# Two halves of a filter unit multiplied at once, and transposes of 16 frequencies instead of 8

## The chip, the cores and the metric

The kernel runs on one core of a Trainium2 chip. A core has five engines that work side by side, each with its own queue of instructions carried out in order: TensorE (PE in the profile; its weight loads are listed apart as PEld), VectorE (DVE), ScalarE (ACT), GpSimd (POOL) and SyncE (SP), from whose queue most transfers between HBM and the on-chip memory SBUF are issued. [...] The metric is the time of one execution on the device in microseconds (us). Lower is better.

## The reference

Four layers act on x, 2048 rows (positions) by 512 channels, in float32. Each adds to x a function of the layer norm of x.

```python
x = x + _A_ref(_layernorm(x), A_w_r, A_w_i)
x = x + _B_ref(_layernorm(x), B_log_A_real, B_A_imag, B_C_real, B_C_imag, B_log_dt, B_D_skip)
x = x + _A_ref(_layernorm(x), A_w_r, A_w_i)
x = x + _B_ref(_layernorm(x), B_log_A_real, ...)

def _A_ref(x, w_r, w_i):                      # a filter in two-dimensional frequency space
    X = jnp.fft.rfft2(x, axes=(-2, -1)) * (w_r + 1j * w_i)
    return jnp.fft.irfft2(X, s=(S, D), axes=(-2, -1))

def _B_ref(u, log_A_real, A_imag, C_real, C_imag, log_dt, D_skip):
    dt = jnp.exp(log_dt)
    A = -jnp.exp(log_A_real) + 1j * A_imag
    C = (C_real + 1j * C_imag) * dt[:, None]
    P = jnp.exp((A * dt[:, None])[:, :, None] * pos)      # channel x mode x position
    K = 2.0 * jnp.einsum("dn,dnl->dl", C, P).real         # the filter from 128 modes
    ...                                                   # causal convolution of u with K by FFT
    return y + u * D_skip
```

The filter K of layer B is the same in both B layers. It has 2048 positions for each of 512 channels, and each value is a sum over 128 modes of a magnitude (a real exponential) times a cosine.

## The kernel before

All Fourier transforms are matrix products on TensorE, split into stages with small factors. The program computes the first A layer, then the first B layer in four blocks of 128 channels, then the second A layer and the second B layer. The filter K is made once, beside the first A layer and the first B layer, and its spectrum is kept for the second.

**The filter.** `kernel_time` goes through 32 units of 16 channels each; the 128 modes lie on the partitions. A position is written as a sum of a coarse and a fine part with 32 values each, so that a unit needs only factors of 16 channels x 32 values, and TensorE multiplies them out. A unit is worked in two halves of 8 channels. Its steps:

- `grow` (line 804), once a unit: three rows of magnitudes, `mag` with 3 x 512 elements, by exponentials on ScalarE and one product on GpSimd.
- `bend` (829), for each half: TensorE puts the phases into a PSUM bank (`pk`, two banks), VectorE rounds them (line 838), TensorE subtracts the whole turns (line 839).
- `sine` (842) and `cosine` (849), for each half: ScalarE takes the absolute value into `kf`, then a sine of the phase and a sine of the absolute value into a tile `qp` of 2 x 3 x 256 elements. All ScalarE work of these steps is recorded with one line, 800, that of the helper `ordered`, which also keeps their order.
- `terms` (853), for each half: VectorE makes two products of 256 elements (line 857, one reads its sine backwards) and one in place of 1024 elements (line 859) with the magnitudes.
- `total` (861), for each half: 16 small matmuls into the one PSUM bank `pv` (line 870), and a copy by ScalarE into `stage` (line 878). Full stages go to HBM.

The units are taken in groups of four (`GROUP`). Within a group the halves follow each other; `terms` lags `sine` by one half (`LAGT`), `total` by four (`LAGV`). After each group come the exponentials of the next, which need another table on ScalarE. `QP = 5` is the number of `qp` buffers, `MAG = 4` that of the magnitudes.

**The transposes.** `forward_b` (line 625) is the forward transform of a block of 128 channels, used for the filter itself (`kernel_freq`) and for the input of each B layer. `rows` makes 64 frequencies for all positions and ScalarE copies them out (line 648); `turn` (line 651) transposes eight of the 64 frequencies with one VectorE instruction of 512 elements (line 654); `pair` (line 659) runs the next matmuls of the helper `side_by_side` (line 316), each pair from 32 frequencies. `weigh` multiplies with the kept spectrum (line 962 from PSUM, line 974 sums of two SBUF tiles on VectorE or GpSimd), `back` transforms back.

**The order.** The lists of steps are dealt into each other by `interleave`, by fractions of each list: filter steps between steps of the layers. `layer_b` holds the transposes of the next block back in two halves of four, so that the first half stands at the end of one block and the second at the start of the next. On top of this written order a scheduler decides, when the program is built, in which order each engine's queue gets its instructions. Tiles come from pools with a fixed number of buffers; who takes a buffer waits for the last reader of its former content.

Of the kernel before, what the change touches and what calls it, by code (L numbers as in the profile page):

```python
# [11 lines left out]
ACT = mybir.ActivationFunctionType  # L12
ALU = mybir.AluOpType
# [36 lines left out]
WE2 = 'g'  # L50
MAG = 4
TH = 2
QP = 5
KF = 1
PM = '2,3,0'
WB = 7
# [190 lines left out]
class Net:  # L247
# [377 lines left out]
    def forward_b(self, src, T, tag="z", extra=None):  # L625


        nc = self.nc
        tiles = {}

        def rows(n0):


            if n0 == 0:
                tiles["z"] = self.sb("z", [64, 2, 2, 8, 2])
            xs = [src(n0 + i) for i in range(4)]
            ps = [self.ps("p1", [64, 2, 2, 2]) for b in range(2)]
            products = [(ps[b][64 * c:64 * c + 64, :, j, m], xs[2 * m + c][64 * b:64 * b + 64, 64 * j:64 * j + 64],
                         T[64 * b:64 * b + 64, n0 + 2 * m + c].rearrange("p (u r) -> p u r", r=2))
                        for m in range(2) for j in range(2) for c in range(2) for b in range(2)]  # L640
            if extra and n0 == 0:
                e = extra()
                for j in (1, 0):
                    products.insert(4 * j + 1, (ps[0][0:64, :, j, 0], e[:, 64 * j:64 * j + 64], products[0][2], True))
            self.side_by_side(products)
            m = n0 // 2
            for b in range(2):
                nc.scalar.copy(tiles["z"][:, :, :, b, m:m + 2].rearrange("p u j m r -> p (u j) (m r)"),  # L648
                               ps[b].rearrange("p u j m r -> p (u j) (m r)"))

        def turn(u):
            if u == 0:
                tiles["zt"] = self.sb(tag, [64, 2, 32])
            nc.vector.transpose(tiles["zt"][:, u:u + 8].rearrange("p u j d -> p (u j d)"),  # L654
                                tiles["z"][:, u:u + 8].rearrange("p u j b m r -> p (u j b m r)"))

        MB = split(self.small[:, 0:256], "slm", [2, 2, 64])

        def pair(i, use):
            last = None  # L660
            for pl in range(2):
                p = self.ps("p2", [512])
                products = []
                for h in (1, 0):
                    o = p[64 * h:64 * h + 64].rearrange("p (u d) -> p u d", d=32)
                    u = 32 * (i % 2) + 16 * h
                    c = 1 if u == 0 else 0
                    z = tiles["zt"][:, :, i // 2]
                    products += [(o[:, 0], MB[:, 0, pl], z[:, 0])] * c + [(o[:, c:], MB[:, 1, pl], z[:, u + c:u + 16])]
                last = self.side_by_side(products, last)  # L670
                use(pl, p)
            self.paired = last

        return ([partial(rows, n0) for n0 in range(0, 16, 4)], [partial(turn, u) for u in range(0, 64, 8)],
                [partial(pair, i) for i in range(4)])

    def exp(self, x, tmp):
# [99 lines left out]
    def kernel_time(self, parts, kt, units, group):  # L777

        nc = self.nc
        BF = mybir.dt.bfloat16  # L780
        TAU = 6.283185
        half = self.half
# [3 lines left out]
        live = {}  # L786
# [9 lines left out]
        def ordered(*a, **k):  # L796
            with ExitStack() as stack:
                if "x" in last:
                    stack.enter_context(self.tc.issue_after(last["x"]))
                last["x"] = nc.scalar.activation(*a, **k).ins  # L800

        last = {}
# [38 lines left out]

        def sine(i, j):
            p, mag = live[i, j]
            QP, f = self.sb("qp", [2, 3, 8, 32]), self.sb("kf", [512])
            ordered(f, p, ACT.Abs)
            ordered(QP[:, 1, 1:3].rearrange("p k d b -> p (k d b)"), p, ACT.Sin, scale=-TAU)
            live[i, j] = f, mag, QP

        def cosine(i, j):
            f, mag, QP = live[i, j]  # L850
            ordered(QP[:, 0, 1:3].rearrange("p k d b -> p (k d b)"), f, ACT.Sin, bias=half, scale=-TAU)

        def terms(i, j):
            f, mag, QP = live[i, j]
            m = mag[:, :, 256 * j:256 * j + 256].rearrange("p k (d b) -> p k d b", b=32)
            for c in (1, 0):
                nc.vector.scalar_tensor_tensor(QP[:, c, 0], QP[:, c, 1, :, ::-1], -1.0 if c else 1.0, m[:, 0], op0=ALU.mult, op1=ALU.mult)  # L857
            t = QP[:, :, 1:3].rearrange("p c k d b -> p c k (d b)")
            nc.vector.tensor_mul(t, t, mag[:, None, 1:3, 256 * j:256 * j + 256].to_broadcast([128, 2, 2, 256]))  # L859

        def total(i, j):

            h = i % 2
            QP = live.pop((i, j))[2]
            p = self.ps("pv", [2, 2, 64])
            for g in range(2):
                for c in range(2):
                    for t in range(2):
                        d = 4 * t + 2 * g
                        nc.tensor.matmul(p[64 * t:64 * t + 64, g], QP[:, c, 2, d:d + 2].rearrange("p s a -> p (s a)"),  # L870
                                         QP[:, c, 0:2, d:d + 2].rearrange("p k s b -> p s k b"),
                                         start=c == 0, stop=c == 1, tile_position=(0, 64 * t), skip_group_check=True)
            blk, ch = i // 8, i // 2 % 4
            if ch % 2 == 0 and h == 0 and j == 0:
                state["stage"] = self.sb("stage", [2, 64, 16])
            stage = state["stage"]
            k = 8 * (ch % 2) + 4 * h + 2 * j
            (nc.vector.tensor_copy if VC[(2 * i + j) % len(VC)] == "v" else nc.scalar.copy)(stage[:, :, :, k:k + 2], p.rearrange("p g s b -> p s b g"))  # L878
            if ch % 2 == 1 and h == 1 and j == 1:
                for t in range(4):  # L880
                    d = 128 * blk + 32 * t + 16 * (ch // 2)
                    self.dma("T")(kt.rearrange("(a b) d -> a b d", b=64)[:, :, d:d + 16],
                                      stage[32 * t:32 * t + 32, t % 2])
# [57 lines left out]
    def layer_b(self, kf, T, out, x=None, src=None, first=None, more=(), fill=(), switch=(), kept=None, fetch=None, after=None):  # L941
# [3 lines left out]
        nc = self.nc  # L945
# [68 lines left out]
            chain.insert(at, (None, *m))  # L1014
        if first is None:
            interleave(chain[0][1])
            interleave(chain[0][2][:4])
        turns = chain[0][2][4:] if first is None else []
        last = []
        fill = [*fill, *[[]] * len(chain)]  # L1020
        for i, (blk, _, _, pairs) in enumerate(chain):
# [9 lines left out]
            if tail:  # L1031
# [2 lines left out]


            steps = [[now[0], *turns, *last[:2]], [now[1], *last[2:4], *then[1][:1], *last[4:6]],
                     [now[2], *last[6:], *then[1][1:2], *units[:2]], [now[3], *units[2:4], *then[1][2:], *then[2][:4]]]
            turns, last = then[2][4:], [*units[4:], *rows]
            steps = sum(steps, [])
            half = len(steps) // 2  # L1040
            part = fill[i][:len(fill[i]) // 2], fill[i][len(fill[i]) // 2:]
# [2 lines left out]
            if tail:  # L1044
                keep = chain[-2][3]
                interleave(turns)
                interleave(chain[-2][1])
                interleave(last[:4])
                interleave(chain[-2][2][:4])
                fetch()  # L1050

                blk, _, _, pairs = chain[-1]
                now = [partial(weigh, blk, pairs, i, YC) for i in range(4)]
                interleave([keep[0], *chain[-2][2][4:], now[0], *last[4:6], keep[1], now[1], *last[6:], keep[2], now[2]])
# [42 lines left out]
def net_kernel(ctx, tc, x, w, ends, kin, log_dt, d_skip, out, **cst):  # L1097
# [15 lines left out]
    with ExitStack() as outer:  # L1113
        with ExitStack() as early:
            early.enter_context(net.phase("pk", P, pk=(2048, PK), pv=(2048, PV)))
            with net.phase("p", P, p1=(2048, 8 - PK - PV), p2="p1", p3="p1"), \
# [3 lines left out]
                with net.phase("m", side="right", raw=(8192, 1), val=(10240, 1), tmp=(14336, 1), hp=(5120, 2)):  # L1120
# [2 lines left out]
                    interleave(A[0][PC:], made)  # L1123
                net.end_weights(ends)
                early.enter_context(net.phase("k", side="right", kb=(5120, 1), ni=(256, 1), kw=(1024, 2), th=(1536, TH), mag=(6144, MAG),
                                              qp=(6144, QP), kf=(2048, KF), stage=(8192, 1)))
                K, marks = net.kernel_time(parts, kt, list(range(32)), GROUP)
                K = ahead(tc, K, KP)
                cuts = [round(f * len(K)) for f in FILL]
# [97 lines left out]
```

## Time and profile before

| | |
|---|---|
| runs, us | 785.32, 784.34, 794.32 |
| median, us | 785.32 |
| span of the profiled execution, us | 781.1 (its own time is given as this span only) |
| DVE busy | 649.3 us (83%) |
| PE busy, mean granted clock | 627.7 us (80%), 0.934 |
| ACT busy | 428.1 us (55%) |
| POOL busy | 404.9 us (52%) |

The profile is of one execution. Busy time is the time in which an engine had at least one instruction under way; for PE it includes waiting inside the matmul pipeline. A group of instructions is given with its line, engine, operation, written and read tiles, shapes and count, then busy time in us and the mean of one in ns, then the engine's idle time just before these instructions and who ended it. A row such as "A <- B: 6.9, 8, 1.9" in the list of waits reads: A waited for B 6.9 us in all, 8 times, at most 1.9 us at once. In the table of stretches each engine has its busy time in that stretch and, in brackets, how many instructions.

### The profile page before, as it was taken

How to read it: one execution, taken by the hardware profiler on the slowest of the kernel's cores; microseconds unless marked ns; L12 is line 12 of the kernel's file. 1: busy time of each engine (PE TensorE's matmuls, PEld its weight loads, DVE VectorE, ACT ScalarE, POOL GpSimd, SP SyncE). 2: the span in 40 equal slices, each digit the busy share in tenths (PEclk: the TensorE clock that was granted, in tenths of full speed). 3: DMA queues.
4: the chain of work that ended last, by engine and by line, in shares of the span. 5: the costliest groups of instructions: out<-in, count | busy, mean ns of one | idle time of the engine just before them, and what ended most of it. 6: DMA issues, size and time to landing. Idle time of an engine off the chain costs nothing. (4 is left out here: it accounts for less than half of the span.)

```text
span 781.1 us, 18929 instructions
## 1 busy us (share of the span) xinstructions
PE 627.7 (80%) x7248; PEld 443.5 (57%) x7248; DVE 649.3 (83%) x1301; ACT 428.1 (55%) x919; POOL 404.9 (52%) x596
## 2 busy tenths in 40 slices
PE   3447888897867977998889887874899896989986
PEld 2336666665534543656365656654777663566766
DVE  7998748979998999769996997878578696889992
ACT  3433778854748765887568834323756336242312
POOL 3675876764825245721657266281055572475760
PEclk9998899999979997999989999997999999799998
DMA  8300552344546503452325539422133114234513
GB/s 311 128 0 1 129 138 56 110 75 151 114 167 184 137 9 64 124 145 82 51 68 117 192 55 257 141 95 69 55 82 83 28 28 136 70 95 120 154 29 83
DMA packets 144923, 80.64 MB, mean 103 GB/s; under 512 B 78561, under 2 KB 124513, under 8 KB 143937
## 3 DMA queue, kind: packets, MB, share of 16 engines
q1 hardware_dynamic: 144576, 78.90, 36.2%
q8 instruction: 58, 0.95, 0.5%
q0 software_dynamic: 256, 0.52, 0.4%
q14 instruction: 33, 0.26, 0.1%
HBM read 54.89 MB, written 25.03 MB: 102 GB/s over the span
## 5 line engine op out<-in xcount | busy, mean ns | idle before, releaser
L974 POOL TENSOR_TENSOR u<-wb,wb 64x512 f32<-64x512 f32 x90 | 129.2, 1436 | 85.2 <-DVE wb L962 75.9
L316 PE MATMUL p<-z,mb 128*64 128x512 f32 (+2 forms) x480 | 102.0, 535 | 8.3 <-DVE wb L962 5.4
L870 PE MATMUL pv<-qp 128*64 128x128 f32 x1024 | 78.9, 295 | 11.4 <-DVE qp L859 6.9
L859 DVE TENSOR_TENSOR qp<-qp,mag 128x1024 f32<-128x1024 f32 x64 | 83.8, 1317 | 1.0
L962 DVE TENSOR_TENSOR wb<-p,kk 128x512 f32<-128x512 f32 x128 | 80.6, 674 | 4.7 <-PE p L316 4.6
L870 PEld LDWEIGHTS pv<-qp 128*64 128x64 f32 x1024 | 62.0, 147 | 38.8 <-ACT stage L878 10.2
L648 ACT COPY z<-p 128x512 f32<-128x512 f32 x96 | 51.4, 597 | 58.1 <-PE p L316 43.7
L316 PE MATMUL p<-mb,u 128*64 128x64 f32 x2048 | 72.9, 235 | 10.6 <-DVE u L974 4.5
L316 PEld LDWEIGHTS p<-mb,u 128*64 128x64 f32 x2048 | 70.7, 150 | 18.7 <-issue 11.3
L857 DVE SCALAR_TENSOR_TENSOR qp<-qp,mag 128x256 f32<-128x256 f32 x128 | 64.8, 523 | 13.6 <-ACT qp L800 13.3
L654 DVE STREAM_TRANSPOSE z<-z 128x512 f32<-128x512 f32 x96 | 58.5, 673 | 18.0 <-ACT z L648 18.0
L527 DVE TENSOR_TENSOR w<-wt,p 128x514 f32<-128x514 f32 x64 | 42.6, 686 | 33.3 <-PE p L316 18.6
L1086 POOL TENSOR_SCALAR w<-w,norms 128x128 f32<-128x128 f32 x64 | 40.5, 647 | 51.9 <-DMA w<-h 28.3
L532 POOL TENSOR_TENSOR w<-w,w 64x257 f32<-64x257 f32 x48 | 40.1, 835 | 50.3 <-DVE w L527 46.2
L456 PE MATMUL p<-w,w 128*128 128x128 f32 x128 | 32.0, 429 | 40.8 <-DVE w L449 30.8
L987 ACT COPY u<-p 128x512 f32<-128x512 f32 x64 | 37.6, 590 | 43.8 <-PE p L316 43.8
L316 PEld LDWEIGHTS p<-z,mb 128*64 128x64 f32 x480 | 34.2, 140 | 37.0 <-issue 20.2
L456 PEld LDWEIGHTS p<-w,w 128*128 128x128 f32 x128 | 27.8, 318 | 44.7 <-issue 24.8
L800 ACT ACTIVATE kf<-pk 128x512 f32<-128x512 f32 x64 | 38.9, 608 | 24.1 <-PE pk L839 23.6
L316 PE MATMUL p<-t,w 64*64 64x128 f32 x1024 | 43.3, 290 | 5.8 <-issue 2.6
L974 DVE TENSOR_TENSOR u<-wb,wb 64x512 f32<-64x512 f32 x38 | 46.9, 1234 | 0.5
L800 ACT ACTIVATE qp<-kf,half 128x512 f32<-128x512 f32 x64 | 47.2, 737 | 0.1
(200 smaller groups left out, 1495.3 us busy)
## 6 DMA issues: line engine op xcount, KB each, us to landing
wt<-in_w SPq DMA_DIRECT2D x32, 257.0 KB
kf<-kk SPq DMA_DIRECT2D x32, 256.0 KB
kk<-kf SPq DMA_DIRECT2D x32, 256.0 KB
u<-in_x SPq DMA_DIRECT2D x16, 256.0 KB
hr<-in_x SPq DMA_DIRECT2D x16, 256.0 KB
kt<-stage SPq DMA_DIRECT2D x32, 128.0 KB
h<-hr SPq DMA_DIRECT2D x16, 256.0 KB
w<-kt SPq DMA_DIRECT2D x32, 128.0 KB
```

The lines of the kernel that those rows point to most:

```text
L316: last = self.nc.tensor.matmul(out, weights, data, start=not more, stop=True, skip_group_check=True).ins
L456: nc.tensor.matmul(p[:, b], xf[:, b], t, start=True, stop=True)
L527: nc.vector.tensor_mul(m[pl], W, px[:, None, :].to_broadcast([128, 2, 257]))
L648: nc.scalar.copy(tiles["z"][:, :, :, b, m:m + 2].rearrange("p u j m r -> p (u j) (m r)"), ps[b].rearrange("p u j m r -> p (u j) (m r)"))
L654: nc.vector.transpose(tiles["zt"][:, u:u + 8].rearrange("p u j d -> p (u j d)"), tiles["z"][:, u:u + 8].rearrange("p u j b m r -> p (u j b ...
L800: last["x"] = nc.scalar.activation(*a, **k).ins
L857: nc.vector.scalar_tensor_tensor(QP[:, c, 0], QP[:, c, 1, :, ::-1], -1.0 if c else 1.0, m[:, 0], op0=ALU.mult, op1=ALU.mult)
L859: nc.vector.tensor_mul(t, t, mag[:, None, 1:3, 256 * j:256 * j + 256].to_broadcast([128, 2, 2, 256]))
L870: nc.tensor.matmul(p[64 * t:64 * t + 64, g], QP[:, c, 2, d:d + 2].rearrange("p s a -> p (s a)"), QP[:, c, 0:2, d:d + 2].rearrange("p k s b ...
L962: nc.vector.tensor_mul(split(m[c, pl], "du", [32, 16]), by_channel(p), split(k[c], "du", [32, 16]))
L974: self.added = e[0].tensor_sub(y[0:64], v[0, 0], v[1, 1]), e[1].tensor_add(y[64:128], v[0, 1], v[1, 0])
L1086: (self.nc.gpsimd if XNE[k] == "g" else self.nc.vector).tensor_scalar(t[:, k], t[:, k], scale, bias, op0=ALU.mult, op1=ALU.add)
```

## The change

Two edits. In the filter, both halves of a unit now share one `qp` tile of 2 x 3 x 512 elements. `sine` and `cosine` still run for each half and write their part of it; `terms` does nothing at the first half and at the second multiplies the whole unit: two products of 512 elements and one of 2048. `total` still runs for each half, on its part of the tile. There are three `qp` buffers of twice the size instead of five. In the transform, `turn` transposes 16 frequencies with one instruction of 1024 elements, and the lists of turns that the order deals out have half as many entries (two and two instead of four and four).

```diff
-QP = 5
+QP = 3
...
         def turn(u):
...
-            nc.vector.transpose(tiles["zt"][:, u:u + 8].rearrange("p u j d -> p (u j d)"),
-                                tiles["z"][:, u:u + 8].rearrange("p u j b m r -> p (u j b m r)"))
+            nc.vector.transpose(tiles["zt"][:, u:u + 16].rearrange("p u j d -> p (u j d)"),
+                                tiles["z"][:, u:u + 16].rearrange("p u j b m r -> p (u j b m r)"))
...
-[partial(turn, u) for u in range(0, 64, 8)]
+[partial(turn, u) for u in range(0, 64, 16)]
...
         def sine(i, j):
             p, mag = live[i, j]
-            QP, f = self.sb("qp", [2, 3, 8, 32]), self.sb("kf", [512])
+            if j == 0:
+                live[i, "qp"] = self.sb("qp", [2, 3, 512])
+            QP, f = live[i, "qp"], self.sb("kf", [512])
             ordered(f, p, ACT.Abs)
-            ordered(QP[:, 1, 1:3].rearrange("p k d b -> p (k d b)"), p, ACT.Sin, scale=-TAU)
+            ordered(QP[:, 1, 1:3, 256 * j:256 * j + 256], split(p, "kd", [2, 256]), ACT.Sin, scale=-TAU)
             live[i, j] = f, mag, QP

         def cosine(i, j):
             f, mag, QP = live[i, j]
-            ordered(QP[:, 0, 1:3].rearrange("p k d b -> p (k d b)"), f, ACT.Sin, bias=half, scale=-TAU)
+            ordered(QP[:, 0, 1:3, 256 * j:256 * j + 256], split(f, "kd", [2, 256]), ACT.Sin, bias=half, scale=-TAU)

         def terms(i, j):
+            if j == 0:
+                return
             f, mag, QP = live[i, j]
-            m = mag[:, :, 256 * j:256 * j + 256].rearrange("p k (d b) -> p k d b", b=32)
+            by_d = lambda t: t.rearrange("p (d b) -> p d b", b=32)
             for c in (1, 0):
-                nc.vector.scalar_tensor_tensor(QP[:, c, 0], QP[:, c, 1, :, ::-1], -1.0 if c else 1.0, m[:, 0], op0=ALU.mult, op1=ALU.mult)
-            t = QP[:, :, 1:3].rearrange("p c k d b -> p c k (d b)")
-            nc.vector.tensor_mul(t, t, mag[:, None, 1:3, 256 * j:256 * j + 256].to_broadcast([128, 2, 2, 256]))
+                nc.vector.scalar_tensor_tensor(by_d(QP[:, c, 0]), by_d(QP[:, c, 1])[:, :, ::-1], -1.0 if c else 1.0, by_d(mag[:, 0]),
+                                               op0=ALU.mult, op1=ALU.mult)
+            t = QP[:, :, 1:3]
+            nc.vector.tensor_mul(t, t, mag[:, None, 1:3].to_broadcast([128, 2, 2, 512]))

         def total(i, j):
-            QP = live.pop((i, j))[2]
+            QP = live.pop((i, j))[2].rearrange("p c k (d b) -> p c k d b", b=32)[:, :, :, 8 * j:8 * j + 8]
...
-            interleave(chain[0][2][:4])
-        turns = chain[0][2][4:] if first is None else []
+            interleave(chain[0][2][:2])
+        turns = chain[0][2][2:] if first is None else []
...
-                                              qp=(6144, QP), kf=(2048, KF), stage=(8192, 1)))
+                                              qp=(12288, QP), kf=(2048, KF), stage=(8192, 1)))
```

The other places where `layer_b` cuts a list of turns change in the same way, from 4 to 2.

More of the change, by code (lines that the diff above doesn't have):

```diff
@@ L672, in pair @@
             self.paired = last
-        return ([partial(rows, n0) for n0 in range(0, 16, 4)], [partial(turn, u) for u in range(0, 64, 8)],
+        return ([partial(rows, n0) for n0 in range(0, 16, 4)], [partial(turn, u) for u in range(0, 64, 16)],
                 [partial(pair, i) for i in range(4)])
@@ L1036, in layer_b @@
             steps = [[now[0], *turns, *last[:2]], [now[1], *last[2:4], *then[1][:1], *last[4:6]],
-                     [now[2], *last[6:], *then[1][1:2], *units[:2]], [now[3], *units[2:4], *then[1][2:], *then[2][:4]]]
-            turns, last = then[2][4:], [*units[4:], *rows]
+                     [now[2], *last[6:], *then[1][1:2], *units[:2]], [now[3], *units[2:4], *then[1][2:], *then[2][:2]]]
+            turns, last = then[2][2:], [*units[4:], *rows]
             steps = sum(steps, [])
@@ L1048, in layer_b @@
                 interleave(last[:4])
-                interleave(chain[-2][2][:4])
+                interleave(chain[-2][2][:2])
                 fetch()
@@ L1053, in layer_b @@
                 now = [partial(weigh, blk, pairs, i, YC) for i in range(4)]
-                interleave([keep[0], *chain[-2][2][4:], now[0], *last[4:6], keep[1], now[1], *last[6:], keep[2], now[2]])
+                interleave([keep[0], *chain[-2][2][2:], now[0], *last[4:6], keep[1], now[1], *last[6:], keep[2], now[2]])
                 units, rows = back(blk)
```

## The prediction

> **What bounds the kernel now.** I read the head of the page first, then a table of stretches, then the groups of VectorE (DVE) instructions, and last single stretches of the timeline. The chain that ended last came first only to be set aside: it covers the last 110 us, where the filter is long made.
>
> ```profile
> span 781.1 us, 18929 instructions
> PE 627.7 (80%) x7248; PEld 443.5 (57%) x7248; DVE 649.3 (83%) x1301; ACT 428.1 (55%) x919; POOL 404.9 (52%) x596
> ...
> PE 7%; DVE 5%; issue 2%; ACT 0%; DVEq 0%; ACTq 0%
> ```
>
> DVE is the busiest engine, TensorE (PE) stands right behind it. A mean over 781 us does not say which of them sets the pace where the change acts, so the next view cuts the part in which the filter is made (line 857's products run from 123.9 to 454.1 us, by a row quoted below) into stretches. The columns are the stretch, its length, and the busy time of each engine.
>
> ```profile
> core 0: us, PE busy (x) PEld busy (x) DVE busy (x) ACT busy (x) POOL busy (x), PEclk, DMA share, GB/s
> 116.00:160.00 44.00, 39.58 (x338) 29.26 (x338) 36.20 (x54) 37.75 (x87) 31.01 (x61) 0.96 0.25 76
> 160.00:240.00 80.00, 64.43 (x418) 40.38 (x418) 76.93 (x176) 46.37 (x90) 37.71 (x58) 0.89 0.47 128
> 240.00:280.00 40.00, 35.07 (x460) 20.70 (x459) 33.73 (x92) 32.58 (x64) 14.51 (x24) 0.96 0.56 149
> 280.00:320.00 40.00, 30.87 (x298) 17.69 (x298) 38.46 (x54) 22.04 (x41) 25.68 (x20) 0.83 0.25 48
> 320.00:360.00 40.00, 38.01 (x573) 25.95 (x572) 29.63 (x58) 33.24 (x65) 15.19 (x25) 1.00 0.52 138
> 360.00:400.00 40.00, 30.54 (x332) 16.83 (x331) 37.94 (x63) 26.39 (x49) 18.03 (x17) 0.94 0.27 56
> 400.00:440.00 40.00, 37.72 (x582) 26.20 (x583) 32.46 (x51) 32.14 (x63) 20.03 (x25) 0.93 0.49 131
> 440.00:480.00 40.00, 33.20 (x532) 23.45 (x531) 36.15 (x66) 17.18 (x35) 27.48 (x30) 0.91 0.54 129
> ```
>
> Two kinds of stretch alternate. In 160-240, 280-320, 360-400 and 440-480 (200 us together) DVE is busy 90 to 96% and PE about 80%: DVE sets the pace. In the other four (164 us) PE is busy 88 to 95%, ACT 80 to 86%, DVE 74 to 84%: there DVE work has cover, and a gain on DVE is worth nothing. Now the groups that the change touches (busy time, mean of one, idle time before them):
>
> ```profile
> L859 DVE TENSOR_TENSOR qp<-qp,mag 128x1024 f32<-128x1024 f32 x64 | 83.8, 1317 | 1.0
> L857 DVE SCALAR_TENSOR_TENSOR qp<-qp,mag 128x256 f32<-128x256 f32 x128 | 64.8, 523 | 13.6 <-ACT qp L800 13.3
> L654 DVE STREAM_TRANSPOSE z<-z 128x512 f32<-128x512 f32 x96 | 58.5, 673 | 18.0 <-ACT z L648 18.0
> ```
>
> They hold 207 of DVE's 649 us. The elements stay the same; what the change can save is what an instruction costs beside its elements.
>
> **The change part by part.** Removed: 64 of 128 short products (line 857), 32 of 64 long ones (line 859), 48 of 96 transposes (line 654): 144 instructions. Each survivor has twice the elements. What is one instruction worth? In a stretch without idle time the distance from start to start tells, not the duration, because neighbours overlap:
>
> ```profile
> 226.71 0.75 DVE L857 SCALAR_TENSOR_TENSOR qp<-qp,mag 128x256 f32<-128x256 f32 x2
> 227.38 0.68 DVE L339 BATCH_NORM_STATS2 bst<-hr 128x6 f32<-128x512 f32 x1
> ...
> 228.04 1.21 DVE L859 TENSOR_TENSOR qp<-qp,mag 128x1024 f32<-128x1024 f32 x1
> 229.18 0.67 DVE L601 TENSOR_TENSOR hr<-hr,p 128x512 f32<-128x512 f32 x1
> ...
> 331.32 4.86 DVE L654 STREAM_TRANSPOSE z<-z 128x512 f32<-128x512 f32 x8 [3.84 <-ACT z L648]
> ```
>
> Two short products take 227.38 - 226.71 = 0.67 us, 0.335 each; a long one 1.14. Then (1.14 - 0.335) / 768 elements = 1.048 ns an element, and 0.067 us is fixed. The transposes agree: 4.86 / 8 = 0.61 = 512 x 1.048 ns + 0.07. So the pure saving is 144 x 0.067 = 9.6 us of DVE time. The new pieces should take 0.60 us (short product, 512 elements), 2.21 (long, 2048) and 1.14 (transpose, 1024) from start to start.
>
> [...]
>
> Second, a wait. The view of one line gives shortest, median and longest duration in ns, and the first and last start:
>
> ```profile
> L857 DVE SCALAR_TENSOR_TENSOR qp<-qp,mag x128: 378/414/1495, 123.9 to 454.1; 128x256 f32<-128x256 f32 x128
> ...
> L859 DVE TENSOR_TENSOR qp<-qp,mag x64: 1185/1218/2301, 126.8 to 454.5; 128x1024 f32<-128x1024 f32 x64
> ```
>
> The means lie above the medians: 128 x (523 - 414) + 64 x (1317 - 1218) ns = 14.0 + 6.3 = 20.3 us are waits of single products. Where they arise:
>
> ```profile
> 295.20 4.32 POOL L974 TENSOR_TENSOR u<-wb,wb 64x512 f32<-64x512 f32 x3
> ...
> 297.17 1.22 DVE L857 SCALAR_TENSOR_TENSOR qp<-qp,mag 128x256 f32<-128x256 f32 x1 [1.51 <-ACT qp L800]
> 298.31 0.68 DVE L838 TENSOR_SCALAR kw<-pk 128x512 bf16<-128x512 f32 x1
> 298.92 0.89 DVE L857 SCALAR_TENSOR_TENSOR qp<-qp,mag 128x256 f32<-128x256 f32 x1
> 299.83 1.23 DVE L859 TENSOR_TENSOR qp<-qp,mag 128x1024 f32<-128x1024 f32 x1
> ```
>
> GpSimd (POOL) runs three sums of 1.44 us from 295.20 to 299.52. Each short product, which reads two SBUF tiles, ends about 0.3 us after one of those sums ends (298.08 and 299.52); the rounding of line 838, which reads PSUM, takes its usual 0.68. So a two-SBUF product waits out the GpSimd instruction under way. Half as many products meet half as many such waits if each product meets one by chance (10.1 us less), and no fewer if the GpSimd instructions are what is met (0 less). I take the first, since the waits fall on single products between other DVE work, and keep zero for the range.
>
> Of this, what lies in the DVE-paced stretches counts. Busy time there, of line 857, of line 859 and of the transposes:
>
> ```profile
> sum 200.00, DVE 37.31; mean DVE 9.33
> ...
> sum 200.00, DVE 43.46; mean DVE 10.87
> ...
> sum 200.00, DVE 12.06; mean DVE 3.02
> ```
>
> The shares are 37.31/64.8 = 0.58, 43.46/83.8 = 0.52, 12.06/58.5 = 0.21. Fixed part: (64 x 0.58 + 32 x 0.52 + 48 x 0.21) x 0.067 = 4.3 us. Waits: 7.0 x 0.58 + 3.2 x 0.52 = 5.7 us. Together -10.0 us. Behind the gain, PE at 80% comes next in those stretches, so 10 of 200 us fits under it.
>
> Third, what the merged form makes later. Products of a unit now begin only when the cosine of its second half is there, and one long product holds DVE 2.21 - 1.14 = 1.07 us longer at a time. Behind it on DVE's queue wait the roundings (line 838), for them PE's last phase matmul, for that ACT's next absolute value; and the sums on PE (line 870) wait for the product itself.
>
> ```profile
> ACT stage L878 <- PE pv L870: 33.9, 26, 4.8
> ...
> ACT kf L800 <- PE pk L839: 23.6, 21, 2.8
> ...
> PE pv L870 <- DVE qp L859: 6.9, 8, 1.9
> PE pk L839 <- DVE kw L838: 6.7, 7, 2.1
> ```
>
> In the built order a rounding stands directly behind a long product 13 times of 64 before and 10 times after. Bounds: nothing where other queued work fills the time; 10 x 1.07 = 10.7 us if each delay ends late. PE's waits on these two DVE results are rare now (15 in all, 0.9 us each), so I take a quarter, +2.7 us. The buffers cost nothing: three of two halves let ACT run as far ahead of PE's sums as five of one half (the sine of half n waited for the sums of half n-5; now the sine that opens unit i+3 waits for those of unit i, and its second half waits for nothing). ACT, PE, GpSimd and the DMA queues issue the same instructions as before, 921, 4010 and 601 on the first three; DMAs on SP change places by a few. At the four points where layer two's blocks begin, the built orders have emitted 32, 48, 64, 64 roundings before and 32, 49, 64, 64 after, so no work changes its stretch.
>
> Behind 480 us only transposes change. On the chain that ended last a block's transposes stand with two pieces or three (start, length):
>
> ```profile
> 667.32 1.20 DVE z L654 x2
> ```
>
> A block needs its second 16 frequencies first; four transposes of 0.60 are now two of 1.14, -0.13 us for each of four blocks: -0.5 us.
>
> Sum: -10.0 + 2.7 - 0.5 = -7.8 us. The profiled span becomes 773.3 us. The median of the runs, 785.3, lies 4.2 above the span; the profile gives no total for its own execution beside the span, and I keep that 4.2: 777.5, rounded to 777.
>
> **The rivals.** *Nothing gained* (780 to 788): GpSimd's instructions are met anyway, only 4.3 + 0.5 us come, and delays eat most: 785.3 - 4.8 + 2.7 = 783. For it: GpSimd is busy for 109 of the 200 DVE-paced us by the stretches. Against it: an undisturbed run of products has no such waits, and two of three instructions disappear from a half at once.
>
> *The whole saving comes through* (762 to 771): DVE sheds 9.6 + 10.1 = 19.7 us and all of it shortens the span, 785.3 - 19.7 = 766. For it: engines wait for each other in turns, and a DVE that is ahead may start PE earlier everywhere. Against it: 164 us with PE at 88 to 95%.
>
> *Slower: the unit waits for its second half* (788 to 810). The work is dealt in 8 groups of four units with a change of ACT's table between; each group's first sums now start one half later, and its last product ends 1.07 + 0.27 us later, while the next exponentials wait for the magnitude buffer that this product reads. A half lasts (454.1 - 123.9)/64 = 5.2 us. If that opening is uncovered in half of the groups, it costs 4 x 5.2 = 20.8 us, less the gains of 10.0 + 0.5 gives 785.3 + 10.3 = 796; in all eight, 816. It decides as soon as more than two groups are uncovered. For it: ACT already waits 33.9 us for sums. Against it: layer work is interleaved in every group.
>
> *GpSimd becomes late* (about 786 to 790): each of 32 long products can hold a GpSimd instruction 1.07 us longer. If eight such delays end PE's wait in the folding stage (160-240), 8.6 us eat the gain. [...] GpSimd's 48% idle time speaks against a loss.
>
> That the change does not do what it says can be left out: the built program has 64, 32 and 48 of the three instructions.
>
> **How the numbers follow.** Forecast (771 to 780): 0.45. Nothing gained, with GpSimd late: 0.25. Whole saving: 0.12. Slower by the second half: 0.18, two thirds of it above 801. A measurement of this kernel tells about 2% from no change: 769.6 and 801.0. Below: most of the third case, 0.10. Above: 0.12. Between: 0.78. The range leaves out the lower end of the third and the upper half of the fourth: 765 to 800.
>
> **What would show it.** Short products near 0.68 us and long ones near 2.28, undisturbed; their excess over this near 10 us in all; DVE busy time down 18 to 22 us; DVE-paced stretches shorter by some 5%, the others unchanged; and the time after 540 us within 1 us. Wrong it would be if PE's and ACT's waits for products and roundings rise by more than 10 us, or if the excess stays at 20 us.

## The result

The changed kernel is slower: 804.49 us median (801.35 to 809.31, 6 runs) against 786.73 us (779.09 to 794.32, 6 runs) for the kernel before; the ratio is 1.0274 [1.0228, 1.032]. The forecast was 777 us, its range 765 to 800.

First the head of the page of the changed kernel, with the span and the busy time of each engine:

```profile
span 804.7 us, 18753 instructions
PE 637.9 (79%) x7247; PEld 451.4 (56%) x7248; DVE 631.2 (78%) x1157; ACT 429.3 (53%) x919; POOL 417.2 (52%) x596
```

DVE does its work in 631.2 us instead of 649.3, with 144 instructions fewer, and yet the span of the profiled execution is 23.6 us longer (the medians lie 17.8 us apart). The groups of DVE instructions that the change touches, and the roundings behind them (busy time, mean of one in ns, idle time before them and who ended it):

```profile
L654 DVE STREAM_TRANSPOSE z<-z 128x1024 f32<-128x1024 f32 x48 | 55.6, 1212 | 26.9 <-ACT z L648 26.7
L864 DVE TENSOR_TENSOR qp<-qp,mag 128x2048 f32<-128x2048 f32 x32 | 74.1, 2316 | 0.8
L838 DVE TENSOR_SCALAR kw<-pk 128x512 bf16<-128x512 f32 x64 | 43.0, 680 | 29.2 <-PE pk L836 29.2
L861 DVE SCALAR_TENSOR_TENSOR qp<-qp,mag 128x512 f32<-128x512 f32 x64 | 51.0, 818 | 12.8 <-ACT qp L800 12.7
```

The view of one line, for the two products (shortest, median and longest duration in ns, first and last start):

```profile
L861 DVE SCALAR_TENSOR_TENSOR qp<-qp,mag x64: 649/685/1756, 130.1 to 469.2; 128x512 f32<-128x512 f32 x64
L864 DVE TENSOR_TENSOR qp<-qp,mag x32: 2267/2285/3025, 133.4 to 470.8; 128x2048 f32<-128x2048 f32 x32
```

The instructions are as short as forecast. Their waits for GpSimd come to 64 x (818 - 685) + 32 x (2316 - 2285) ns = 9.5 us, 20.3 before. So nothing went wrong with these instructions themselves; the time is lost elsewhere. The table of stretches of the changed kernel, at four places (the same columns as before):

```profile
160.00:240.00 80.00, 63.30 (x432) 42.72 (x431) 66.03 (x139) 45.07 (x89) 42.83 (x63) 0.93 0.44 113
280.00:320.00 40.00, 29.15 (x223) 15.38 (x223) 35.92 (x42) 21.70 (x39) 23.84 (x17) 0.74 0.20 35
320.00:360.00 40.00, 34.37 (x529) 23.44 (x523) 23.55 (x27) 29.88 (x59) 16.84 (x23) 0.91 0.47 124
400.00:440.00 40.00, 28.13 (x420) 19.68 (x421) 29.84 (x31) 25.12 (x49) 26.34 (x24) 0.87 0.33 82
```

In 160-240 DVE is busy 66.03 of 80 us, 76.93 before: room, but no earlier end. In 400-440 no engine is busy three quarters of the time, where PE had 37.72 of 40: engines wait for each other in turns. A fixed cut doesn't compare shifted kernels, so the next table cuts at line 962 (967 after), the products with the filter's spectrum, 16 to a block: at the end of the first, 17th, 33rd and 49th of them.

| part, us | before | after |
|---|---|---|
| until the first block's products | 285.2 | 284.8 |
| first block to second | 91.7 | 106.5 |
| second to third | 85.9 | 93.4 |
| third to fourth | 33.7 | 37.0 |
| from there to the end | 284.7 | 282.9 |

Units 0 to 15 and the folding of the filter lose nothing, the layers after the filter nothing; the blocks beside which units 16 to 31 are made lose 25.6 us. Each column is one execution, and differences of a few us mean nothing: E4 below, whose VectorE order is that of the kernel before, takes 4.6 us longer up to the first block. The list of waits of the changed kernel:

```profile
ACT stage L883 <- PE pv L875: 45.2, 31, 6.5
ACT kf L800 <- PE pk L839: 35.7, 25, 4.5
DVE kw L838 <- PE pk L836: 29.2, 13, 8.3
PE pk L839 <- DVE kw L838: 12.1, 9, 4.0
```

Against 33.9, 23.6, 1.6 and 6.7 before. All four have grown; which of them costs time, only experiments tell.

### The profile page after: what moved, and what is told of

The parts are those of the page before. It is cut to its first block, busy times and chain, and to the rows that moved or that the text cites. A ratio compares the mean times of both kernels' runs of the same rounds, so it can differ in the third digit from the quotient of the medians.

```text
span 804.7 us, 18753 instructions
## 1 busy us (share of the span) xinstructions
PE 637.9 (79%) x7247; PEld 451.4 (56%) x7248; DVE 631.2 (78%) x1157; ACT 429.3 (53%) x919; POOL 417.2 (52%) x596
## 5 line engine op out<-in xcount | busy, mean ns | idle before, releaser
L979 POOL TENSOR_TENSOR u<-wb,wb 64x512 f32<-64x512 f32 x90 | 135.9, 1510 | 113.5 <-DVE wb L967 105.6
L316 PE MATMUL p<-z,mb 128*64 128x512 f32 (+1 forms) x480 | 104.2, 542 | 6.6 <-DVE wb L967 3.3
L875 PEld LDWEIGHTS pv<-qp 128*64 128x64 f32 x1024 | 65.1, 153 | 33.6 <-issue 15.0
L654 DVE STREAM_TRANSPOSE z<-z 128x1024 f32<-128x1024 f32 x48 | 55.6, 1212 | 26.9 <-ACT z L648 26.7
L864 DVE TENSOR_TENSOR qp<-qp,mag 128x2048 f32<-128x2048 f32 x32 | 74.1, 2316 | 0.8
L532 POOL TENSOR_TENSOR w<-w,w 64x257 f32<-64x257 f32 x48 | 44.0, 916 | 51.8 <-DVE w L527 47.9
L1091 POOL TENSOR_SCALAR w<-w,norms 128x128 f32<-128x128 f32 x64 | 36.9, 589 | 56.6 <-DMA w<-h 48.8
L838 DVE TENSOR_SCALAR kw<-pk 128x512 bf16<-128x512 f32 x64 | 43.0, 680 | 29.2 <-PE pk L836 29.2
L861 DVE SCALAR_TENSOR_TENSOR qp<-qp,mag 128x512 f32<-128x512 f32 x64 | 51.0, 818 | 12.8 <-ACT qp L800 12.7
L800 ACT ACTIVATE kf<-pk 128x512 f32<-128x512 f32 x64 | 38.5, 602 | 36.7 <-PE pk L839 35.7
L316 PEld LDWEIGHTS p<-z,mb 128*64 128x64 f32 x480 | 35.0, 141 | 37.6 <-issue 20.2
L979 DVE TENSOR_TENSOR u<-wb,wb 64x512 f32<-64x512 f32 x38 | 50.3, 1323 | 0.7
```

Source lines behind the costliest of these rows:

```text
L316: last = self.nc.tensor.matmul(out, weights, data, start=not more, stop=True, skip_group_check=True).ins
L532: e[0].tensor_sub(Y[0:64, v], m[0][hs, 0], m[1][hs, 1])
L654: nc.vector.transpose(tiles["zt"][:, u:u + 16].rearrange("p u j d -> p (u j d)"), tiles["z"][:, u:u + 16].rearrange("p u j b m r -> p (u j ...
L838: nc.vector.tensor_scalar(whole, p, MAGIC, -MAGIC, op0=ALU.add, op1=ALU.add)
L861: nc.vector.scalar_tensor_tensor(by_d(QP[:, c, 0]), by_d(QP[:, c, 1])[:, :, ::-1], -1.0 if c else 1.0, by_d(mag[:, 0]), op0=ALU.mult, op1= ...
L864: nc.vector.tensor_mul(t, t, mag[:, None, 1:3].to_broadcast([128, 2, 2, 512]))
```

## The experiments

All ratios are to the kernel before, with 95% intervals; points are per cent of its time.

**One edit at a time.** E1 has the merged products with transposes of 8, E2 the transposes of 16 with products by halves.

```diff
 E1: QP = 3, sine, cosine, terms, total as changed;  turn(u): u:u + 8, as before
 E2: turn(u): u:u + 16, lists of turns cut at 2;     QP = 5, kernel_time as before
```

> The products for both halves at once, transposes of 8 frequencies as before. If the loss comes from the products (late start, long instruction or buffers): ratio to before 1.02 to 1.03, VectorE's wait for its rounding near 29 us. If it comes from the transposes: 1.00, wait near 2 us.

> Only the transposes of 16 frequencies; products and buffers as before. If the transposes do the harm: 1.02 or more. If the products do it: 0.995 to 1.00, with some 3 us of VectorE time saved, of which 0.5 to 1.5 us show behind 540 us.

E1 measured 1.011 [1.0071, 1.0149], E2 1.0025 [0.9991, 1.0058]. The products lose by themselves, though less than the 1.02 expected. The transposes alone can't be told from no change, but both together lose 1.4 points more than the sum.

**Late, or merged?** E4 keeps the shared tile of a unit, three buffers, and makes the products of each half at their old place. E3 also has products of the old size, but the first half's are issued behind the second half's.

```diff
 E4:
+        def terms(i, j):
+            half_terms(i, j)          # 2 products of 256, 1 of 1024, on half j of the tile
 E3:
+            if j == 0:
+                return
+            half_terms(i, 0, half_terms(i, 1))
```

> One tile for a unit, products of the old sizes (256 and 1024 elements), but those of the first half issued behind those of the second. Tells late start from long instruction. Late start (the first half's products wait for the second half's cosine): 1.02 to 1.035, a little worse than the merged products, since the 144 fewer instructions are not had. Long instruction (one product holds VectorE 2.2 us): 1.00 to 1.01.

> One tile for a unit and three buffers of it, products of the old sizes at their old places; VectorE's order is that of the kernel before. Buffers or the shared tile as the cause: 1.02. Late start or long instruction as the cause: 1.00.

E3 measured 1.0326 [1.0291, 1.036], E4 0.9984 [0.9938, 1.0031]. So three big buffers cost nothing, and a late start with 128 + 64 products and no merged instruction costs 3.4 points, about 27 us. From E3 to E1 the merging gives 2.1 points back, about 17 us. Not all of this need be the saving: E3's order also makes PE wait longer for the products, as its list of waits shows:

```profile
PE pv L886 <- DVE qp L869: 16.2, 14, 3.8
```

The same wait is 6.9 us before and 3.0 in E1.

**At the ends of a group?** Groups of four units with a change of ACT's table between (1283 ns for one load at line 800 of the kernel before, 16 in all) were the place that the prediction's slower rival named. E5 makes the first unit of each group by halves and merges the others, E6 does that with the last unit, E7 with both.

```diff
+            if i % group == 0:                  # E5;  E6: group - 1;  E7: in (0, group - 1)
+                return half_terms(i, j)
```

> Transposes of 8. The first unit of each group of four makes its products half by half as before; the other three units at once. If the harm lies in the opening of a group (no products to do before the second half's cosine): the 1.011 of the merged products falls to 1.000 or below. If it lies in the closing (the magnitudes and sums of the last unit come late): it stays near 1.011. If every unit pays alike: a quarter comes back, 1.008.

> Transposes of 8. Only the last unit of each group half by half, the other three at once. Closing: 1.000 or below. Opening: near 1.011. Every unit alike: 1.008.

> Transposes of 8. First and last unit of each group half by half, the two in the middle at once. Opening and closing together: 0.993 to 0.998, below the kernel before, since the middle units keep half of the saved instructions. Every unit alike: 1.005.

Measured: E5 1.0083 [1.0048, 1.0119], E6 1.0151 [1.0105, 1.0197], E7 1.0152 [1.0102, 1.0202]. The intervals of E5 and E6 both hold E1's 1.011, so neither end of a group can be told from nothing, and E7, which merges only two units of four, is no faster than E1: it missed both of the values expected. The loss doesn't come back with the openings and closings, and it isn't a sum over units.

**Which units?** E9 merges units 0 to 15 and leaves 16 to 31 by halves, E10 the other way round.

```diff
+            if i >= 16:                         # E9;  E10: i < 16
+                return half_terms(i, j)
```

> Transposes of 8. Units 0 to 15, whose products mostly lie beside the first A layer, at once; units 16 to 31, beside the blocks of the B layer, half by half. If merging pays where the filter has slack and costs only in the blocks, where each block waits for its filter: 0.993 to 0.999. If the cost is spread over all units: 1.005.

> The other way round: units 16 to 31 at once, units 0 to 15 half by half. Cost in the blocks only: 1.012 to 1.018, all of it between the first and the last spectrum product of the first B layer. Cost spread over all units: 1.005.

E9 measured 0.9972 [0.993, 1.0014], E10 1.0176 [1.0127, 1.0226]. The loss belongs to units 16 to 31, beside the blocks, as the table of parts said: in E10's profiled execution (794.76 us, below its median of 801.61) the three parts from the first block to the fourth take 12.8 us longer than before, the whole span 11.8. In E10 it can be watched. From the timeline of E10, VectorE (start, length, and in brackets the idle time before with its releaser):

```profile
315.43 1.26 DVE L990 TENSOR_TENSOR u<-wb,wb 64x512 f32<-64x512 f32 x1
316.62 3.41 DVE L872 SCALAR_TENSOR_TENSOR qp<-qp,mag 128x512 f32<-128x512 f32 x2
320.07 2.29 DVE L875 TENSOR_TENSOR qp<-qp,mag 128x2048 f32<-128x2048 f32 x1
322.28 1.28 DVE L838 TENSOR_SCALAR kw<-pk 128x512 bf16<-128x512 f32 x2
328.97 1.30 DVE L872 SCALAR_TENSOR_TENSOR qp<-qp,mag 128x512 f32<-128x512 f32 x2 [5.41 <-ACT qp L800]
```

And from E10's timelines of GpSimd, TensorE and ScalarE in the same window:

```profile
314.88 4.61 POOL L990 TENSOR_TENSOR u<-wb,wb 64x512 f32<-64x512 f32 x3 [4.14 <-DVE wb L978]
...
323.02 0.59 PE L839 MATMUL pk<-kw,ni 128*128 128x512 bf16 x1 [7.04 <-DVE kw L838]
...
323.70 0.60 ACT L800 ACTIVATE kf<-pk 128x512 f32<-128x512 f32 x1 [7.29 <-PE pk L839]
```

PE's phases (lines 835 and 836) had been issued by 314.1. The roundings that they wait for stand on DVE's queue behind three products: the two short ones take 3.41 us instead of 1.30, because they meet GpSimd's three sums, the long one 2.29. In that time PE's queue stands at line 839, and the matmuls of the back transform stand behind it, though they need no rounding and GpSimd's last sum for them was ready at 319.49. ACT has nothing to do until the phases come; then DVE, with its products done, waits 5.41 us for ACT's sines. One delay is paid by three engines in a row. At this place the kernel before has a single rounding between products, and on PE's queue the 64 matmuls of the back transform stand ahead of line 839; from the timelines of its VectorE and TensorE:

```profile
317.10 0.67 DVE L838 TENSOR_SCALAR kw<-pk 128x512 bf16<-128x512 f32 x1
...
318.79 1.50 DVE L857 SCALAR_TENSOR_TENSOR qp<-qp,mag 128x256 f32<-128x256 f32 x1
320.21 0.67 DVE L838 TENSOR_SCALAR kw<-pk 128x512 bf16<-128x512 f32 x1
...
316.64 3.46 PE L316 MATMUL p<-mb,u 128*64 128x64 f32 x64 [0.70 <-ACT u L983]
320.04 0.53 PE L839 MATMUL pk<-kw,ni 128*128 128x512 bf16 x1
```

So PE's order changed here too, and no run tests that by itself.

The changed kernel shows the same one block later, where the roundings stand behind the short products; the timeline of its VectorE:

```profile
416.44 3.42 DVE L861 SCALAR_TENSOR_TENSOR qp<-qp,mag 128x512 f32<-128x512 f32 x2
419.79 1.27 DVE L838 TENSOR_SCALAR kw<-pk 128x512 bf16<-128x512 f32 x2
...
436.97 1.29 DVE L838 TENSOR_SCALAR kw<-pk 128x512 bf16<-128x512 f32 x2 [8.29 <-PE pk L836]
438.18 4.61 DVE L654 STREAM_TRANSPOSE z<-z 128x1024 f32<-128x1024 f32 x4
```

and its TensorE:

```profile
420.51 1.19 PE L839 MATMUL pk<-kw,ni 128*128 128x512 bf16 x2 [3.96 <-DVE kw L838]
```

**Roundings first.** If the order on DVE's queue is the cause, merged products should cost nothing once the rounding stands ahead of them. E12 is E1 with each unit's short products issued only behind the newest rounding; E12A is the same on the changed kernel, with transposes of 16. E15 puts the same rule on the kernel before. The rule is two edits: `LAGT = 2` deals the products out one half later, and `issue_after` holds the short ones back. They were not tried apart.

```diff
-LAGT = 1
+LAGT = 2
...
-            nc.vector.tensor_scalar(whole, p, MAGIC, -MAGIC, op0=ALU.add, op1=ALU.add)
+            last["round"] = nc.vector.tensor_scalar(whole, p, MAGIC, -MAGIC, op0=ALU.add, op1=ALU.add).ins
...
+                with self.tc.issue_after(last["round"]):
                     nc.vector.scalar_tensor_tensor(...)
```

> Products at once, transposes of 8; each unit's products are issued on VectorE only behind the newest rounding, so that no rounding stands behind a late product. If the loss is the rounding behind the products (TensorE's queue stands, ScalarE has no phases): 0.995 to 1.003 in place of 1.011, VectorE's wait for products' sines grows instead. If it is the late start itself: 1.011 or more.

> The same on the changed kernel with its transposes of 16. Rounding behind products as the cause: 1.000 to 1.010 in place of 1.027. Late start: 1.025.

> The kernel before, whose products are also issued only behind the newest rounding. If putting roundings ahead is worth something by itself: 0.985 to 0.99, and the products at once with roundings ahead would still lose beside it. If it only mends what the late products do: 1.00 to 1.01, since here products that are ready are held back.

E12 measured 0.9986 [0.9952, 1.002], E12A 1.003 [0.9998, 1.0063], E15 1.0263 [1.022, 1.0305]. The loss is gone, in E12 from 1.011 and in E12A from 1.0274. One thing came out against the expectation: VectorE's wait for the products' sines, 9.5 us in E1 and 12.7 in the changed kernel, didn't grow in E12 but vanished. So the rule changes two things at once, what stands behind late products and VectorE's waiting in front of them, and E12 alone doesn't tell which of them counts; the kernel before has 13.3 us of the second and loses nothing. It isn't that this order is better for any kernel: on products by halves it costs 2.6 points, more than either value expected. Why it costs there wasn't tried; such a product waits for a rounding 64 times instead of 32, and ACT waits 44.9 us for PE's phases, longer than in the changed kernel. Under the same rule the merged form is 1.0263 / 0.9986, 2.8 points or 22 us, the shorter one. E12's list of waits:

```profile
ACT stage L884 <- PE pv L876: 53.1, 37, 6.5
DVE kw L838 <- PE pk L836: 23.9, 15, 4.0
ACT kf L800 <- PE pk L839: 20.2, 20, 4.2
...
PE pk L839 <- DVE kw L838: 5.6, 5, 1.9
```

The conspicuous new wait, DVE for PE's phases (29.2 us after, 1.6 before), stays at 23.9 in a kernel that loses nothing, and ACT's wait for the sums even grows: neither total follows the loss. The two that fall back are PE's for the rounding and ACT's for PE behind it (35.7 after, 23.6 before, 20.2 here). The latter in the list of waits of E4, which loses nothing either:

```profile
ACT kf L800 <- PE pk L839: 23.2, 25, 2.5
```

and in that of E1:

```profile
ACT kf L800 <- PE pk L839: 40.4, 26, 6.9
```

Totals over the whole run don't settle it: E2 loses nothing measurable with 30.5 us of this wait and 10.2 of PE's for the rounding, and E6 loses 1.5 points with 30.3 and 6.7. The list of PE's waits over the first two blocks alone separates better. The row of PE's wait for the rounding there, of the kernel before, the changed kernel and E10, in this order:

```profile
PE pk L839 <- DVE kw L838: 3.9, 4, 2.1
PE pk L839 <- DVE kw L838: 10.1, 6, 4.0
PE pk L839 <- DVE kw L838: 12.6, 6, 7.0
```

In the first two blocks of E12 it is 2.6 us and of E9 3.4, without a loss; of E1 6.9 and of E15 8.9, with one; only E2 has 6.2 without one. Directly this wait is 6 of the 25.6 us that the blocks lose. PE also waits longer there for ACT's sines to free a phase bank (4.8 us before, 9.5 after) and for transfers of the filter (1.5 and 6.4), and from the first block to the fourth it is busy 189.5 us instead of 178.0. That all of this follows from the roundings is argued, not shown.

The corresponding place of E12 in the timelines of its VectorE and TensorE:

```profile
323.84 1.27 DVE L838 TENSOR_SCALAR kw<-pk 128x512 bf16<-128x512 f32 x2
325.04 1.27 DVE L862 SCALAR_TENSOR_TENSOR qp<-qp,mag 128x512 f32<-128x512 f32 x2
326.34 3.25 DVE L865 TENSOR_TENSOR qp<-qp,mag 128x2048 f32<-128x2048 f32 x1
...
324.56 0.38 PE L839 MATMUL pk<-kw,ni 128*128 128x512 bf16 x1 [1.09 <-DVE kw L838]
```

The long product still takes 3.25 us, but PE waits 1.09 us and not 7.04.

**Another way out: a third phase bank.** If PE's phases were merely too few ahead, a third `pk` bank would help (one bank is taken from the other matmul results for it).

```diff
-PK = 2
+PK = 3
...
-PM = '2,3,0'
+PM = '2,2,0'
```

> The kernel before with three phase banks instead of two, and one bank less for each of two stages of the transforms. A base for the next run; 1.00 to 1.03 for the bank that the transforms lose.

> Products at once, transposes of 8, three phase banks. If the two banks tie rounding, sine and product into a ring that the late products stretch: at or below the run before, a loss of 0 instead of 1.1 per cent. If the banks play no part: 1.011 times the run before.

With three banks the kernel before measured 1.0133 [1.0092, 1.0175], E1's products 1.0295 [1.0251, 1.034]. The merged form still loses 1.0295 / 1.0133 = 1.016: the number of banks is not what the loss hangs on.

**What the transposes add.** E8 is the changed kernel with lists of turns of the old length, every second one empty.

```diff
         def turn(u):
+            if u % 16:
+                return
...
-[partial(turn, u) for u in range(0, 64, 16)]
+[partial(turn, u) for u in range(0, 64, 8)]
```

> Products at once and transposes of 16, as in the changed kernel, but the lists that the order deals out keep eight entries of transposes, every second one empty. If the transposes harm through the places that the shorter lists give to the filter's steps (roundings of the next group ahead of the transposes near 430 us): 1.010 to 1.015 in place of 1.027. If through their length: 1.027.

It measured 1.0225 [1.016, 1.0291], between E1 and the changed kernel, and its interval overlaps that of the latter: this settles nothing. In its trace the four transposes of that block stand ahead of the next roundings again (at 433.92, as in E1 at 433.28; after: 438.18). That with the roundings first both sizes of transposes are alike (E12, E12A) suggests that most of the 1.4 points hangs on the late products too.

**Versions that might beat both.** E11 is E9 with transposes of 16 in the second B layer alone, E16 is E12 with the same, and E17 is E12 with the rule on units 16 to 31 alone.

```diff
 E11, E16:
+    def forward_b(self, src, T, tag="z", extra=None, n=8):      # n=16 where layer two's input is transformed
 E17:
+                    if i >= 16:
+                        stack.enter_context(self.tc.issue_after(last["round"]))
```

> Units 0 to 15 at once as in the run before last, and transposes of 16 frequencies in the second B layer alone, where no filter is made. 1 to 1.5 us below that run: 0.991 to 0.998. If the longer transposes cost by themselves: above it.

> Products at once behind the newest rounding, transposes of 8 beside the filter and of 16 in the second B layer alone: 0.996 to 0.999, some 1 us below the same without the long transposes.

> Products merged, transposes of 8, and a unit's short products issued on VectorE only behind the newest rounding, but for units 16 to 31 alone, those beside the first B layer's blocks. Theory (the late products stand ahead of the rounding only there): units 0 to 15 keep what merging gives them in the built order, so at least as good as the same rule for all units: 0.994 to 0.999 of the kernel before. Rival (the rounding has to come first in the folding stage too): 1.000 to 1.006.

E11 measured 0.9998 [0.9964, 1.0032], E16 1.0032 [1.0002, 1.0062], E17 0.9962 [0.9924, 1.0] (medians of 785.27 us and, before, 785.53). Transposes of 16 gain nothing measurable even where no filter work is about; E11 and E16 both missed the gain of some 1 us. E17 is the best median beside E4's, and not told apart from the kernel before. DVE is busy 631.2 us in E12, 629.0 in E12A and 628.5 in E17, 18 to 21 us less than before, and no version is shorter for it. Whether some lateness that remains eats the saving, or DVE's time is worth nothing there, no run separates.

## Why the prediction was wrong

**What bounds the kernel: right as a reading, too strong as a rule.** The stretches where DVE is busy 90 to 96% were there. But before the first block DVE's busy time fell from 244.4 to 230.7 us, and that part is 284.8 us long instead of 285.2. The scheduler used the room for something else: before the first block PE did 448 of the filter's matmuls (line 870) instead of 480, and the rest moved into block one. That move isn't the loss: E9 has 448 there and loses nothing, E10 has 480 and loses. The sentence "no work changes its stretch" was drawn from the roundings alone and was wrong.

**First and second term, the saving: right on DVE, not seen in the span.** DVE busy -18.1 us, the undisturbed durations and the excess of 9.5 us came as forecast (18 to 22, 0.68, 2.28, about 10). What the span gets of it stays open. The shares by stretches turned 19.7 us into 10.0; from E3 to E1 the merged form gains 17 us and from E15 to E12 22 us, but each of these pairs differs in more than the merging, and E12, with 18.1 us less of DVE's work, is no shorter than the kernel before. Of DVE's 18.1 us, 10.8 are fewer waits of products (20.3 to 9.5). That leaves 7.3 us for 144 instructions, 0.051 us each, where the forecast's fixed part of 0.067 us gave 9.6.

**Third term, what the merged form makes later: this is the step that failed.** It stood at +2.7 us, a quarter of ten times 1.07 us. With the other terms as they stood, -10.0 and -0.5, the 17.8 us between the medians ask for about +28; a late start without merging measures about 27 us (E3 against E4), some of it where PE waits for products before its sums (line 870). Three things were wrong in it. The delay was taken as the 1.07 us by which one long product is longer, but what stands ahead of the roundings is the whole unit's products, 5.7 us in E10 (316.62 to 322.28). The count took only roundings directly behind a long product, while the changed kernel's 419.79 stands behind two short ones. (Counting those too would not have warned: by the traces 36 of 64 roundings stand directly behind a product before and 24 after. Nor does the sum: the time in which a rounding of units 16 to 31 has its phases and a product is running ahead of it, added up over the 32 roundings, falls from 46.8 to 38.7 us. The longest of these delays rises from 4.6 to 5.7.) And the quarter came from PE's waits being rare before, when products of one half filled gaps; the wait of the old order says little about the new one. The bound of 10.7 us that I gave was no bound: it left out the queue behind PE's line 839 and ACT behind that. How large each part of this is, the runs don't show.

**The buffers at nothing: right** (E4). **The transposes at -0.5 us:** the part from the fourth block on is 1.8 us shorter, of the size of the differences between versions that don't differ there; no run tells it from nothing. Beside the merged products the same transposes cost 1.4 points, about 11 us, and the prediction has no term for the two changes together.

**The rivals.** The one on the other side, *the unit waits for its second half*, had the right sign, a range (788 to 810) that holds the result, and the right start of the chain, with a chance of 0.18. Its place was wrong: it looked at the eight openings, where E5 gets back 0.3 of a point, within the noise; the time is lost beside the blocks, as far as E10's rows show it at roundings inside the groups. *GpSimd becomes late* named the folding stage, which lost nothing; that a long product can hold a GpSimd instruction is shown by single sums (last section). *The whole saving comes through* had the size of DVE's saving about right (19.7 us, 18.1 measured), and missed what it costs to get it. *Nothing gained* was wrong in its reason, since the waits for GpSimd did fall, but E12 and E17, with the late start mended, end within its 780 to 788.

**What would show it.** The prediction's own alarm went off: ACT's wait for the phases and its wait for the sums rose by 12.1 and 11.3 us, and PE's for the roundings by 5.4. PE's wait for the products themselves fell, from 6.9 to 2.5.

What is shown: the late start beside the blocks costs the time (E3, E4, E9, E10), and the order that puts short products behind the newest rounding takes the loss away (E12, E12A, E17). What stays open: whether the roundings are the whole of the path or only the part that E10's rows show, which of the two things that the rule in E12 changes does the mending, why the same order costs 2.6 points with products by halves (E15), why transposes of 16 lose 1.4 points only beside late products, and why E5 to E7 don't add up.

## What to carry to other kernels

Merging two instructions can save on its engine what it promises (here 18.1 us of DVE's busy time, 18 to 22 forecast), but its operands are ready only when the later half is: look, on that engine's queue, at what then stands behind the merged block, and follow who waits for it through every engine of the loop, at the full length of the block and not its increase. If something short on the loop's path stands behind, give it its place by an explicit order, and try that with the merge. The wait that grows most in the list need not be the one that costs (here DVE's for PE's phases, 1.6 us before and 23.9 in E12, which loses nothing): compare the list with that of a version that has the change and not the loss.

## What the hardware showed beside this

Two products of 512 elements take 1.30 us when undisturbed and 3.41 us beside three GpSimd sums (E10, rows above), so the same products are cheap or dear by what GpSimd does at that moment. There VectorE waits; in single sums it is GpSimd: a sum of the changed kernel that starts at 286.12 us, 0.2 us after a product of 2048 elements, takes 3.19 us, where the median of the 90 sums is 1.28. In the kernel before one that starts at 286.52 us, 0.2 us after a product of 1024 elements, takes 2.13, with the same median. The mean of the sums says little about the merging: it rises from 1436 ns to 1510 in this group of the changed kernel, but is 1434 in E10, which merges the products beside these sums too:

```profile
L979 POOL TENSOR_TENSOR u<-wb,wb 64x512 f32<-64x512 f32 x90 | 135.9, 1510 | 113.5 <-DVE wb L967 105.6
```

PE is also busier in the changed kernel: with the same matmuls its busy time is 637.9 us against 627.7, the mean granted clock 0.912 against 0.934. In this group of the changed kernel one matmul takes 306 ns, 295 before:

```profile
L875 PE MATMUL pv<-qp 128*64 128x128 f32 x1024 | 81.9, 306 | 4.0 <-DVE qp L864 2.5
```

In E12 the busy time is back at 627.3 us. That waiting lowers the clock is not shown: E9, which loses nothing, was granted 0.912 as well, and so was E10, where the same matmul takes 298 ns.
